# A fused linear attention and gated feed-forward kernel: the attention output x on 64x64 quarters of the array

One core of a Trainium2 chip. The metric is the time of one execution on the device, in microseconds (us); lower is better. The kernel before takes 319.8 us.

## The reference

```python
q_s = softmax(q, axis=-1)                     # [8, 8, 576, 64]: batch, heads, rows, head size
k_s = softmax(k, axis=2)                      # over the rows
kv  = einsum('bhsd,bhse->bhde', k_s, v)       # one 64x64 matrix per head
x   = einsum('bhsd,bhde->bhse', q_s, kv)      # per head, then heads side by side: 4608 x 512
out = (gelu(x @ w_gate) * (x @ w_val)) @ w_out   # 512 -> 1536 -> 512
```

Most of the arithmetic is in the last line. The change concerns `x`, for batches 3 to 7.

## The kernel before

The 576 rows of a batch are split into 512 ("main") and 64 ("left over"; those of all eight batches are run together as a ninth pass). The profile calls the tensor engine PE, its weight loads PEld, VectorE DVE and ScalarE ACT; PSUM is the memory into which matmuls write. Of the tiles named in it, `psg`, `psv` and `psy` are the PSUM results of the gate, value and output products, `pskv` is k times v, `psx` is x of the main rows and `psxr` x of the left-over rows. `eqt` holds the transposed exponentials of q.

Two heads share one full matmul. Their two 64x64 matrices stand on the diagonal of a 128x128 weight, whose other half a mask has set to zero:

```python
def kv_norm(b, g):                      # pskv -> kv_sb, divided by the sums of k, times the mask
    ...
    nc.vector.scalar_tensor_tensor(out=kv_sb, in0=pskv[...], scalar=rck[:, j:j + 1], in1=mask,
                                   op0=ALU.mult, op1=ALU.mult)

def unit_x(b, hp, eng="act", big=False):          # hp: a pair of heads
    xt = get_xt(b)
    psx = (ps_big if big else ps_att).tile([P, MAIN], f32, name="psx", ...)
    nc.tensor.matmul(psx, st[(b, "kv", hp)].rearrange("p h e -> p (h e)"),
                     xq(b, hp), start=True, stop=True)          # 128x128 weight, 512 columns
    copy_on(eng, xt[:, hp, :], psx)

def unit_xrem(b, eng="act"):                      # the 64 left-over columns, four pairs
    psx = ps_att.tile([P, HP, REM], f32, name="psxr", tag="att")
    for hp in range(HP):
        nc.tensor.matmul(psx[:, hp, :], ..., xqr(b, hp), start=True, stop=True)
    copy_on(eng, xtr[:, :, b * REM:(b + 1) * REM], psx)
```

They are placed between the output matmuls of the batch before (`NS, 1` is after the second group of 12 output matmuls, `NS, 12` in the middle of the third, `NS, 2` after it; `FI, 5` and `FI, 7` stand likewise between its gate and value matmuls):

```python
at(b, FI, 5, L(unit_kv, n, 0))
at(b, FI, 7, L(unit_kv, n, 1))
at(b, NS, 1, L(unit_x, n, 0, "dve"), L(unit_x, n, 1, "dve"))
at(b, NS, 2, L(unit_x, n, 2, "act"), L(unit_x, n, 3, "act"))
at(b, NS, 12, L(unit_xrem, n))
```

The softmax here doesn't subtract the row's maximum and nothing guards it: scores larger than these inputs give would overflow.

## Time and profile before

| | before |
|---|---|
| time, median of 4 runs | 319.81 us (319.61 to 320.08) |
| tensor engine (PE) busy | 98% of the span |
| next busiest, VectorE (DVE) | 61% |
| one batch on PE | 33.2 us |
| of that, x: four psx and four psxr | 0.98 us |

The prediction below shows the lines. The time in which PE works on something is read in this document from the first start of it to the first start of what follows; the recorded length of a matmul is not used.

### The profile page before, as it was taken

How to read it: one execution, taken by the hardware profiler on the slowest of the kernel's cores; microseconds unless marked ns; L12 is line 12 of the kernel's file. 1: busy time of each engine (PE TensorE's matmuls, PEld its weight loads, DVE VectorE, ACT ScalarE, POOL GpSimd, SP SyncE). 2: the span in 40 equal slices, each digit the busy share in tenths (PEclk: the TensorE clock that was granted, in tenths of full speed). 3: DMA queues.
4: the chain of work that ended last, by engine and by line, in shares of the span. 5: the costliest groups of instructions: out<-in, count | busy, mean ns of one | idle time of the engine just before them, and what ended most of it. 6: DMA issues, size and time to landing. Idle time of an engine off the chain costs nothing.

```text
span 317.9 us, 4491 instructions
## 1 busy us (share of the span) xinstructions
PE 311.6 (98%) x1658; PEld 148.8 (47%) x1658; DVE 194.1 (61%) x341; ACT 139.8 (44%) x179; POOL 44.7 (14%) x59
## 2 busy tenths in 40 slices
PE   8899999999999999999999999999999999999995
PEld 3444454455545444544454444444444444444444
DVE  3943386698898469747884689457953434234331
ACT  3753565989432753256433653384331233113300
POOL 2667551330004000200003000300000000000000
PEclk9999999999999999999999999999999999999999
DMA  7999999940196118711492139203020210140002
GB/s 231 372 383 395 400 385 388 394 160 0 68 344 215 40 66 268 277 52 66 144 383 70 68 113 386 81 17 132 2 62 22 80 54 0 23 106 6 0 35 99
DMA packets 42342, 50.76 MB, mean 160 GB/s; under 512 B 3408, under 2 KB 38096, under 8 KB 42320
## 3 DMA queue, kind: packets, MB, share of 16 engines
q1 hardware_dynamic: 40592, 48.84, 44.3%
q10 hardware_dynamic: 1728, 1.64, 1.7%
q8 instruction: 13, 0.21, 0.3%
q14 instruction: 9, 0.07, 0.1%
HBM read 37.75 MB, written 9.44 MB: 148 GB/s over the span
## 4 chain that ended last, share of the span: by engine, by line
PE 90%; DMA 4%; ACT 3%; DVE 2%; issue 1%; ACTq 0%
PE psy L436 28%; PE psg L358 27%; PE psv L358 27%; PE pskv L213 2%; DMA out_dram<-yo 2%; PE psx L334 2%; DMA qt<-in_q_dram 2%; PE psl L457 1%; DVE rq L177 1%; ACT eq L150 1%; PE pst L275 1%; DVE eq L186 0%; ACT L363 0%; ACT L150 0%; ACT L353 0%
## 5 line engine op out<-in xcount | busy, mean ns | idle before, releaser
L363 ACT ACTIVATE gl<-psg 128x512 f32<-128x512 f32 x108 | 63.9, 598 | 128.1 <-PE psg L358 125.5
L365 DVE SCALAR_TENSOR_TENSOR ht<-psv,gl 128x512 f16<-128x512 f32 x108 | 72.9, 682 | 63.8 <-PE psv L358 63.2
L358 PE MATMUL psg<-xt,wg_sb 128*128 128x512 f16 x384 | 100.5, 379 | 0.1
L358 PE MATMUL psv<-xt,wv_sb 128*128 128x512 f16 x384 | 100.5, 379 | 0.0
L436 PE MATMUL psy<-wo_sb,ht 128*128 128x512 f16 x420 | 95.6, 379 | 0.0
L358 PEld LDWEIGHTS <-wv_sb 128*128 128x128 f16 x432 | 42.2, 98 | 51.2 <-issue 0.8
L358 PEld LDWEIGHTS <-wg_sb 128*128 128x128 f16 x432 | 41.5, 98 | 47.0 <-issue 0.4
L436 PEld LDWEIGHTS <-ht 128*128 128x128 f16 x420 | 40.5, 98 | 47.1
L485 DVE TENSOR_SCALAR yo<-psy 128x512 f32<-128x512 f32 x30 | 20.6, 689 | 31.3 <-PE psy L436 31.3
L128 POOL CAST v<-vt 128x640 f16<-128x640 f32 x26 | 18.8, 762 | 138.4 <-DMA vt<-in_v_dram 121.4
L167 DVE TENSOR_REDUCE rq<-eq 128x10 f32<-128x640 f16 x28 | 22.7, 812 | 5.4 <-ACT eq L150 5.0
L186 DVE TENSOR_TENSOR eq<-eq,rrq 128x640 f16<-128x640 f16 (+1 forms) x29 | 23.3, 804 | 0.3
L150 ACT ACTIVATE ek<-kt 128x1280 f16<-128x1280 f32 (+1 forms) x11 | 19.1, 1746 | 3.6 <-DMA kt<-in_k_dram 3.6
L150 ACT ACTIVATE eq<-qt 128x2560 f16<-128x2560 f32 (+2 forms) x10 | 18.4, 1862 | 2.3 <-DMA qt<-in_q_dram 2.2
L300 DVE STREAM_TRANSPOSE et<-eq 128x640 f16<-128x640 f16 x20 | 16.9, 845 | 0.7
L130 ACT CAST xt<-psx 128x512 f16<-128x512 f32 x17 | 9.3, 588 | 12.9 <-PE psx L334 12.9
L358 PE MATMUL psg<-xtr,wg_sb 128*128 128x512 f16 x48 | 12.3, 379 | 0.0
L358 PE MATMUL psv<-xtr,wv_sb 128*128 128x512 f16 x48 | 12.3, 379 | 0.0
L350 PE MATMUL pswarm<-warm,ident 128*128 128x512 f16 x34 | 9.9, 452 | 1.4 <-POOL ident masks.py:199 1.4
L213 PEld LDWEIGHTS <-ek 128*128 128x128 f16 x140 | 9.1, 97 | 3.1
L150 ACT ACT_TABLE_LOAD x8 | 10.3, 1283 | 0.6 <-DMA qt<-in_q_dram 0.5
L132 DVE CAST xt<-psx 128x512 f16<-128x512 f32 x15 | 9.7, 681 | 1.2 <-PE psx L334 1.2
(67 smaller groups left out, 133.3 us busy)
## 6 DMA issues: line engine op xcount, KB each, us to landing
out_dram<-yo SPq DMA_DIRECT2D x14, 512.0 KB, 3.1
kt<-in_k_dram SPq DMA_DIRECT2D x7, 640.0 KB, 7.1
vt<-in_v_dram SPq DMA_DIRECT2D x7, 640.0 KB, 8.1
qt<-in_q_dram SPq DMA_DIRECT2D x7, 640.0 KB, 5.8
qt<-in_q_dram SPq DMA_DIRECT2D x8, 512.0 KB, 5.8
eqt<-et SPq DMA_DIRECT2D x80, 40.0 KB, 1.9
wost<-in_moe_w_out_dram SPq DMA_DIRECT2D x6, 512.0 KB, 7.9
kt<-in_k_dram SPq DMA_DIRECT2D x6, 512.0 KB, 7.4
```

The lines of the kernel that those rows point to most:

```text
L128: nc.gpsimd.tensor_copy(out=dst, in_=src)
L150: nc.scalar.activation(out=dst[:, n0:NC, h0 * D:h1 * D].rearrange("p n (h d) -> p h n d", d=D), in_=tiles[(nm, b)][:, h0:h1, n0 * D:NC * D ...
L167: nc.vector.reduce_sum(rq, e, axis=mybir.AxisListType.X)
L186: (nc.gpsimd if eng == "pool" else nc.vector).tensor_tensor(out=e, in0=e, in1=rrq.unsqueeze(-1).to_broadcast((P, n, 2, D)), op=ALU.mult)
L213: nc.tensor.matmul(st[(b, "pskv", g)][:, j, :], ek_b[b % 2][:, n, hp * P:(hp + 1) * P], v16_b[b % 2][:, n, 2 * hp:2 * hp + 2, 0:VW], start ...
L300: nc.vector.transpose(out=et[:, :, hp].rearrange("p c (n i) -> p n c i", i=32), in_=eq_b[b % 2][:, :, hp * P:(hp + 1) * P].rearrange("p n ...
L350: nc.tensor.matmul(ps, ident, warm, start=True, stop=True)
L358: nc.tensor.matmul(ps, w[:, ci, fi * P:(fi + 1) * P], xt[:, ci, :], start=(ci == 0), stop=(ci == HP - 1))
L363: nc.scalar.activation(out=gl, in_=psg, func=ACTF.Gelu)
L365: nc.vector.scalar_tensor_tensor(out=ht, in0=psv, scalar=_H_SCALE, in1=gl, op0=ALU.mult, op1=ALU.mult)
L436: nc.tensor.matmul(psy, hts[fi][:, ns * P:(ns + 1) * P], wo_sb[:, fi, :], start=(fi == 0), stop=(fi == NFI - 1))
L485: nc.vector.tensor_scalar(out=yo, in0=psy, scalar1=1.0 / _H_SCALE, scalar2=None, op0=ALU.mult)
```

## The change

The intent: half of the array multiplies zeros in `unit_x`. Instead, each head gets a quarter of the array, and four heads run at the same time. The two heads of a pair sit on the upper and the lower 64 rows; two pairs take the left and the right 64 columns. How the array is split is called its tiling mode (128*128 and 64*64 in the lines of the trace). So that results come out in the order in which the next product wants them, pairs are now made of heads c and c+4; the exponentials and casts, which copy every element anyway, do that on their way.

```diff
+    def heads(x, b, h0, h1):
+        if b >= T32:                                   # T32 = 3
+            return x.rearrange("p (t c) x -> p c t x", t=2)[:, h0 // 2:h1 // 2]
+        return x[:, h0:h1]
...                                                     # used by exp; cast_v likewise
+    def unit_x4(b):
+        xt = get_xt(b)
+        def go(ps, hp, src):
+            for s in range(2):
+                r, t = slice(64 * s, 64 * s + 64), hp % 2
+                nc.tensor.matmul(ps[s][64 * t:64 * t + 64], st[(b, "kv", hp)][r, s, :], src[r],
+                                 start=True, stop=True)
+        psr = [ps_att.tile([P, 2, REM], f32, name="psxr", tag="att") for _ in range(2)]
+        for hp in range(HP):
+            go([p[:, hp // 2] for p in psr], hp, xqr(b, hp))
+        for s, eng in enumerate(("act", "dve")):
+            copy_on(eng, xtr[:, 2 * s:2 * s + 2, b * REM:(b + 1) * REM], psr[s])
+        for i in range(2):
+            ps = [ps_big.tile([P, MAIN], f32, name="psx", tag="mm") for _ in range(2)]
+            for hp in (2 * i, 2 * i + 1):
+                go(ps, hp, xq(b, hp))
+            for s, eng in enumerate(("act", "dve")):
+                copy_on(eng, xt[:, i + 2 * s, :], ps[s])
...
-                at(b, NS, 1, L(unit_x, n, 0, "dve"), L(unit_x, n, 1, "dve"))
-                at(b, NS, 2, L(unit_x, n, 2, "act"), L(unit_x, n, 3, "act"))
-                at(b, NS, 12, L(unit_xrem, n))
+                at(b, NS, 1, L(unit_x4, n))
```

More of the change, by code (lines that the diff above doesn't have):

```diff
@@ L98 @@
     wo_sb = wpool.tile([P, NFI, C], f16, name="wo_sb")
+    T32 = 3
+    def heads(x, b, h0, h1):
+        if b >= T32:
+            return x.rearrange("p (t c) x -> p c t x", t=2)[:, h0 // 2:h1 // 2]
+        return x[:, h0:h1]
     tiles = {}
@@ L149, in exp @@
         dst = (ek_b if nm == "k" else eq_b)[b % 2]
+        o, i = (("p n (c t d) -> p c t n d", "p c t (n d) -> p c t n d") if b >= T32 else
+                ("p n (h d) -> p h n d", "p h (n d) -> p h n d"))
         nc.scalar.activation(
-            out=dst[:, n0:NC, h0 * D:h1 * D].rearrange("p n (h d) -> p h n d", d=D),
-            in_=tiles[(nm, b)][:, h0:h1, n0 * D:NC * D].rearrange("p h (n d) -> p h n d", d=D),
+            out=dst[:, n0:NC, h0 * D:h1 * D].rearrange(o, d=D, **({"t": 2} if b >= T32 else {})),
+            in_=heads(tiles[(nm, b)], b, h0, h1)[..., n0 * D:NC * D].rearrange(i, d=D),
             func=ACTF.Exp)
     def cast_v(b, h0, h1, eng="pool"):
-        if eng == "pool" and h1 - h0 > 2:
+        if h1 - h0 > 2 and (eng == "pool" or b >= T32):
             for h in range(h0, h1, 2):
-                cast_v(b, h, h + 2)
+                cast_v(b, h, h + 2, eng)
             return
         copy_on(eng, v16_b[b % 2][:, :, h0:h1, 0:D].rearrange("p n h d -> p h n d"),
-                tiles[("v", b)][:, h0:h1, :].rearrange("p h (n d) -> p h n d", d=D))
+                (tiles[("v", b)][:, h0 // 2::4] if b >= T32 else tiles[("v", b)][:, h0:h1]).rearrange(
+                    "p h (n d) -> p h n d", d=D))
     def norm_sum(b, hp, n0=0):
@@ L594 @@
     at(3, FI, 11, L(unit_xrem, 0, "dve"))
-    T32 = 3
     for b in range(2, B):
```

## The prediction

> **What bounds the kernel now.** I read the page's totals first, then the chain that ended last, then the stretch of the trace in which the changed work lies. The totals say that the tensor engine is busy practically all the time, and no other engine is near it:
>
> ```profile
> span 317.9 us, 4491 instructions
> PE 311.6 (98%) x1658; PEld 148.8 (47%) x1658; DVE 194.1 (61%) x341; ACT 139.8 (44%) x179; POOL 44.7 (14%) x59
> ```
>
> The chain that ended last says the same in another way: 90% of it is PE, and the line of x (psx, L334) is 2% of it.
>
> ```profile
> PE 90%; DMA 4%; ACT 3%; DVE 2%; issue 1%; ACTq 0%
> PE psy L436 28%; PE psg L358 27%; PE psv L358 27%; PE pskv L213 2%; DMA out_dram<-yo 2%; PE psx L334 2%; DMA qt<-in_q_dram 2%; PE psl L457 1%; DVE rq L177 1%; ACT eq L150 1%; PE pst L275 1%; DVE eq L186 0%; ACT L363 0%; ACT L150 0%; ACT L353 0%
> ```
>
> A busy PE is not yet a PE at its peak, so the third view is the timeline of PE in one output stage, the one in which x of batch 5 is computed (columns: start, length, instructions):
>
> ```profile
> 174.15 5.34 PE L436 MATMUL psy<-wo_sb,ht 128*128 128x512 f16 x24
> 179.33 0.59 PE L334 MATMUL psx<-eqt,kv_sb 128*128 128x512 f16 x2
> 179.76 1.46 PE L436 MATMUL psy<-wo_sb,ht 128*128 128x512 f16 x6
> 181.05 0.28 PE L341 MATMUL psxr<-eqt,kv_sb 128*128 128x64 f16 x4
> 181.17 1.46 PE L436 MATMUL psy<-wo_sb,ht 128*128 128x512 f16 x6
> 182.47 0.59 PE L334 MATMUL psx<-eqt,kv_sb 128*128 128x512 f16 x2
> 182.90 2.75 PE L436 MATMUL psy<-wo_sb,ht 128*128 128x512 f16 x12
> 185.49 0.81 PE L358 MATMUL psg<-xt,wg_sb 128*128 128x512 f16 x3
> ```
>
> Read starts, not lengths: 24 matmuls of 512 columns from 174.15 to 179.33 are 0.216 us each, while one record lasts 379 ns, because each overlaps the next. From piece to piece there is no gap: the two psx cost 179.76 - 179.33 = 0.43 us, the four psxr 0.12 us, the other two psx 0.43 us. So x of one batch occupies PE for **0.98 us**, and every bit of that is on the path, since PE has nothing idle beside it. The same three pieces with the same distances stand at 112.56, 146.12, 212.54 and 245.75 us. Five batches make 4.9 us, 1.5% of the time. A whole batch checks this: 96 gate and value matmuls and 48 output matmuls at 0.216 are 31.1 us, 20 pskv from 162.64 to 163.21 and again from 166.66 to 167.24 are 1.15 us, and x 0.98 us: 33.2 us, and the window of one batch (174.31 to 207.52) is 33.2 us.
>
> **What the Trainium skill says.**
> (1) "TensorEngine Tiling (Array Packing)", Key Properties: tiles work independently, in weight loads and matmuls; changing the tiling mode drains the tensor engine. Every matmul of the kernel before is 128*128, so its trace can confirm neither; no mode is switched in it.
> (2) "TensorE: Matmul & The Clock Gate", Part 3: matmuls on different tiles overlap, with a span of about one matmul plus some 4 ns for each further tile; four row tiles were measured at 3.07 times, sixteen tiles at 10.6 times. No tiled matmul is in this trace. The same page has a warm 512-column matmul every 216 ns, and this trace has 0.216 us.
> (3) The same page, Fast Weight Load: it needs the full 128 columns; the tiling page adds that column tiling switches it off. A load then takes columns / 1.2 GHz, 53 ns for 64. In this trace a full load is recorded at 98 ns, yet four psxr with their four loads pass in 0.12 us, so loads are pipelined here; without the fast mode this may be worse.
> (4) "Perfetto Trace Analysis", Tensor Engine Instruction: the end of a matmul is an estimate of the profiler. The trace agrees (379 ns against 216 ns from start to start), and their difference, 163 ns, is my measure of how long a drain may last.
>
> **The change, part by part.** For batches 3 to 7 the casts put heads c and c+4 side by side. x of a pair was one 128x128 matmul with a block-diagonal weight, half of whose cells are zeros. It becomes two 64x64 matmuls, one on the upper and one on the lower rows; two pairs fill all four quarters. If four run together, 8 matmuls of 512 columns take the time of two.
> - Removed per batch: 4 psx and 4 psxr, 0.98 us.
> - Added, x itself: two groups of four, 2 x 0.216 = 0.43 us, and about 3 x 0.02 us for the later start of the last tile: 0.49 us.
> - Added, the 64 left-over columns: 8 instead of 4 matmuls. At the 0.03 us of one psxr (0.12 / 4) they look bound by issue and weight loads, not by columns, so I give concurrency nothing here: 8 x 0.03 = 0.24 us. It was 0.12 us.
> - Added, two changes of mode (psy to x, x to psy). A whole drain would be 0.163 us each; part of it should pass beside the next weight load. I choose 0.125 us each, 0.25 us together. This is the least certain term.
> - Sum: 0.49 + 0.24 + 0.25 = 0.98 us, just what was removed. Before the drains it is a gain of 0.25 us per batch, 1.2 us in all.
> - Moved: all of it goes to the end of the second output row group, where the first two psx were. Rotated operands come by the sixteen transposing DMAs, whose issues end at 163.19 + 10.13 = 173.3 us plus 1.9 us to land; x starts at 179.3. For the last batch it is 229.61 + 10.33 + 1.9 = 241.8 against 245.75. No wait there. psxr comes 1.7 us earlier, still behind the data.
> - Buffers: four of the six large PSUM buffers are taken at once. The ring then gives psg and psv of rows 10 and 11, whose readers are done some 5 us before (the last gate product of the batch is at 174.42 + 0.69), and the next output takes the one that was copied out around 177 us. The copies of x end about 3 us before the next batch's first psg at 185.49, so nobody waits for them.
> - Copies: six per batch instead of five (two of 128 columns instead of one of 256, and still two each of 512 on ACT and DVE). DVE gets some 0.3 us more in a stage where it has idle time (0.70 us before the yo at 179.53, 1.35 us before that at 185.69). ACT's exp ends at 179.96, about when the first x is ready, and its copies are then needed by nobody for 5 us. The casts in the new head order have the same elements and counts: exp still takes whole batches (2.33 us), v still goes in 128x640 pieces. All off the path.
>
> **The rivals.** Since PE is bound and nothing else is, the time after is 319.67 + 5 x (X - 0.98), with X what PE spends on x of one batch.
> - Drain costs nothing and the small matmuls overlap too: X = 0.43 + 0.06 + 0.12 = 0.61, -1.9 us, 317.8 us. For it: the page's 4 ns. Against it: the same skill's sentence on the drain.
> - Only two of four run together, say because the two column tiles on the same rows share a stream or the weight loads of 64 columns don't hide (8 x 53 ns = 0.43 us, an estimate from the TensorE page, is as long as the matmuls themselves): X = 4 x 0.216 + 0.24 + 0.33 = 1.43, +2.3 us, 322.0 us. Nothing in this trace speaks against it.
> - No overlap at all: X = 8 x 0.216 + 0.24 + 0.33 = 2.30, +6.6 us, 326.3 us. Against it: the measured speedups on the page.
> - PE waits, as the order of work changed: a PSUM buffer or a DMA as the new bound. The margins above (2 to 5 us) speak against it; a wait of 0.5 us in each batch would make +2.5 us.
> - A larger gain is not there: x removed altogether would give 4.9 us, 1.5%.
>
> **Range and chances.** The sum lands at equal, 319.6 us. Eight in ten I put between the first rival and the second, a little narrower at the bottom because I believe in some drain: 318.0 to 322.2. Faster by over 2% (6.4 us) is impossible by the last bound, unless something unseen moves: 0.01. Slower by over 2% needs no overlap at all, or waits: 0.04. Within 2%: 0.95.
>
> **What would show it.** In the profile after, the psx group should be 64*64, 64x512, twice as many for batches 3 to 7 (40, beside 12 old ones), and PE's timeline should go from psy to psxr, psx and psy without other work between. The distance from the first psxr to the next psy is X: 0.6 to 1.4 us if I am right. Starts of psx that come in bunches of four, a bunch every 0.22 us, prove four at a time; even distances of 0.1 us are pairs, of 0.2 us none. The gap between the last psy before and the first psxr beyond 0.216 us, and that of the last psx to the next psy, are the drains. Gate matmuls and outputs should keep 0.216 us, and a batch outside x its 32.2 us. The prediction is wrong if X is off these numbers, or if PE shows waits on a PSUM copy, on kv_sb or on eqt that were not there.

## The result, and the profile after

| | before | after |
|---|---|---|
| median of 4 runs each | 319.81 us | 318.40 us (318.31 to 318.87) |
| span in the profile | 317.9 us | 316.7 us |
| first start of x to the next psy, batch 5 | (three pieces) 0.98 us | 0.62 us |

The ratio is 0.9958, with a 95% interval of 0.9941 to 0.9976: 1.3 us less. Ratios here are the mean time of one kernel's fast runs over that of the other's fast runs of the same rounds, so not quite the ratio of the medians quoted.

The totals of the page of after:

```profile
span 316.7 us, 4572 instructions
PE 309.7 (98%) x1698; PEld 146.8 (46%) x1698; DVE 195.4 (62%) x346; ACT 138.4 (44%) x179; POOL 44.6 (14%) x59
```

PE is as full as it was and still bounds the kernel. It has 40 more matmuls and is done 1.2 us earlier. The output stage of after in which x of batch 5 is computed (the timeline of PE; start, length, instructions), to be held against the one in the prediction. Two windows of the timeline are put together; the first ends at 179.0, so that it counts only four of the eight psxr:

```profile
173.70 5.34 PE L471 MATMUL psy<-wo_sb,ht 128*128 128x512 f16 x24
178.97 0.22 PE L365 MATMUL psxr<-eqt,kv_sb 64*64 64x64 f16 x4
...
178.97 0.26 PE L365 MATMUL psxr<-eqt,kv_sb 64*64 64x64 f16 x8
179.06 0.60 PE L365 MATMUL psx<-eqt,kv_sb 64*64 64x512 f16 x8
179.59 5.35 PE L471 MATMUL psy<-wo_sb,ht 128*128 128x512 f16 x24
184.78 1.03 PE L393 MATMUL psg<-xt,wg_sb 128*128 128x512 f16 x4
```

The sum can be read off. The 24 psy begin at 173.70 and need 24 x 0.216 = 5.18 us, to 178.88; psxr begins at 178.97, so **0.09 us** is lost on entering. All eight psxr take 179.06 - 178.97 = **0.09 us**. From the first psx to the next psy are 0.53 us, of which two steps of 0.216 are 0.43 us; the rest, **0.10 us**, is lost on leaving. In all 0.71 us where before had 0.98 us: 0.27 us less per batch, 1.35 us in five batches, which agrees with the measured difference. The psx start as the prediction said that four at a time would: in this window four between 179.05 and 179.08, the other four between 179.27 and 179.30. All the rest on PE together has moved by no more than 0.02 us: from the psy that follows x in batch 5 (in before, its first piece) to the same point in the next, after takes 212.55 - 179.59 = 32.96 us and before 212.97 - 179.76 = 33.21 us, 0.25 us more.

The weight loads (PEld) of the same stage show where the two losses lie:

```profile
178.97 0.21 PEld L365 LDWEIGHTS <-kv_sb 64*64 64x64 f16 x16 [0.42 <-issue]
179.59 2.49 PEld L471 LDWEIGHTS <-ht 128*128 128x128 f16 x13 [0.41 <-issue]
```

In before, the loads of the first two psx stand here:

```profile
179.11 0.31 PEld L334 LDWEIGHTS <-kv_sb 128*128 128x128 f16 x2
```

There a load starts well ahead of its matmul (load at 179.11, psx at 179.33). In after the first load of each kind starts only with its own matmul, after some 0.4 us without any load. At each change of mode the overlap is broken.

### The profile page after: what moved, and what is told of

Same layout as the page of the kernel before. It is cut to its first block, busy times and chain, and to the rows that moved or that the text cites. A ratio compares the mean times of both kernels' runs of the same rounds, so it can differ in the third digit from the quotient of the medians.

```text
span 316.7 us, 4572 instructions
## 1 busy us (share of the span) xinstructions
PE 309.7 (98%) x1698; PEld 146.8 (46%) x1698; DVE 195.4 (62%) x346; ACT 138.4 (44%) x179; POOL 44.6 (14%) x59
## 4 chain that ended last, share of the span: by engine, by line
PE 90%; DMA 4%; ACT 3%; DVE 2%; issue 1%; ACTq 0%
PE psy L471 29%; PE psg L393 28%; PE psv L393 28%; PE pskv L226 2%; DMA out_dram<-yo 2%; DMA qt<-in_q_dram 2%; PE psl L492 1%; DVE rq L190 1%; PE psx L365 1%; PE psx L347 1%; ACT eq L162 1%; PE pst L288 1%; DVE eq L199 0%; ACT L398 0%; ACT L162 0%
## 5 line engine op out<-in xcount | busy, mean ns | idle before, releaser
L471 PE MATMUL psy<-wo_sb,ht 128*128 128x512 f16 x420 | 94.3, 379 | 0.0
```

What stands on the lines that cost most here:

```text
L471: nc.tensor.matmul(psy, hts[fi][:, ns * P:(ns + 1) * P], wo_sb[:, fi, :], start=(fi == 0), stop=(fi == NFI - 1))
```

## Experiments

Theory: the gain is four matmuls at the same time on four quarters, less what two changes of mode cost. Rivals: it is the gathering of three pieces into one; it is that a 64x64 matmul is short in itself. Medians of before in the four groups of runs on one chip each are 319.6 to 320.1 us, so ratios are compared.

### The move alone

Full matmuls as before, all at the place where the change has them.

```diff
-at(b, NS, 1, L(unit_x, n, 0, "dve"), L(unit_x, n, 1, "dve"))
-at(b, NS, 2, L(unit_x, n, 2, "act"), L(unit_x, n, 3, "act"))
-at(b, NS, 12, L(unit_xrem, n))
+at(b, NS, 1, L(unit_xrem, n), L(unit_x, n, 0, "act", True), L(unit_x, n, 1, "dve", True),
+   L(unit_x, n, 2, "act", True), L(unit_x, n, 3, "dve", True))
```

> The kernel before, with full 128x128 matmuls, but the four psxr and the four psx of batches 3 to 7 all at the place where the change puts them. Theory (the gain is four matmuls at a time on the quarters): no gain, 319.8 us, ratio 0.999 to 1.001, and psxr plus psx still take 0.98 us from the first start to the next psy. Rival (the gain is from gathering the three pieces in one place): 318.4 us, ratio 0.996.

Measured: 319.71 us, ratio 1.000 (0.9986 to 1.0013). Its PE timeline at the same place:

```profile
177.19 2.32 PE L436 MATMUL psy<-wo_sb,ht 128*128 128x512 f16 x10
179.35 0.28 PE L341 MATMUL psxr<-eqt,kv_sb 128*128 128x64 f16 x4
179.47 1.02 PE L334 MATMUL psx<-eqt,kv_sb 128*128 128x512 f16 x4
180.33 0.59 PE L436 MATMUL psy<-wo_sb,ht 128*128 128x512 f16 x2
```

From 179.35 to 180.33 is 0.98 us, and there is no gap on entering (177.19 + 10 x 0.216 = 179.35). The move gives nothing, and the gaps of after do not come with this place: full matmuls have none there.

### The order of issue

Three kernels issue the same eight psx per batch in other orders, so as to let only two quarters run side by side.

```diff
-for hp in (2 * i, 2 * i + 1):
-    go(ps, hp, xq(b, hp))
+for hp, s in ORDER: ...          # shortened: the same matmul, for pair hp and half s (tile s, hp % 2)
+# e2: (0,0) (0,1) (2,0) (2,1) (1,0) (1,1) (3,0) (3,1)    rows only
+# e3: (0,0) (1,0) (2,0) (3,0) (0,1) (1,1) (2,1) (3,1)    columns only
+# e4: (0,0) (2,0) (1,0) (3,0) (0,1) (2,1) (1,1) (3,1)    each tile twice in a row
```

In these three and in the next three kernels the four PSUM buffers are taken together and the copies stand after all eight psx, where after copies each four.

> The kernel after with the eight psx of a batch in another order: head pair 0, 2, 1, 3, so that only the upper and lower row tiles of one column half can run side by side, and the next two wait for the same two tiles. Theory: four steps of 0.216 us for two, 0.43 us more per batch, 2.2 us in all, 320.6 us, ratio 1.002. Rival (small matmuls pass faster by themselves, or more than four are in flight): 318.4 us, as the kernel after.

> The kernel after with all upper-row matmuls of psx before all lower-row ones, so that only the two column tiles on the same rows can run side by side, each with its own stream of data. Theory: also 0.43 us more per batch, 320.6 us, ratio 1.002. Rival (column tiles on the same rows share one stream, and the speed came from the rows alone): eight steps with an overlap of rows only in the middle, 7 to 8 times 0.216 us, up to 6 us more, 324 us.

> The kernel after with the two matmuls of each quarter right after one another. Theory, with starts in order: the second of a quarter waits for the first, and runs beside the first of the next quarter, so five steps of 0.216 us for two: 0.65 us more per batch, 3.2 us in all, 321.6 us, ratio 1.006. Rival (starts need not be in order, or a quarter need not wait for itself): 318.4 us. Rival (a quarter's second matmul blocks everything until it ends): eight steps, 324.9 us.

Measured: 318.50, 318.71 and 318.72 us; ratios 0.9965, 0.9967 and 0.9965, with intervals between 0.9951 and 0.9981. All three are as fast as after within the interval. The numbers of my theory were missed all three times, and as it stood, a rival's number (318.4 us) had come true. Which one? In e4 the psx of a batch, counted in short stretches (the stretch, its length, then the busy time of PE, with the number of psx that are running by their recorded lengths in brackets; the columns after that are other engines, the clock and DMA):

```profile
179.40:179.45 0.05, 0.00 (x0) 0.00 (x0) 0.00 (x0) 1.00 0.00 0
179.45:179.49 0.04, 0.02 (x4) 0.00 (x0) 0.00 (x0) 1.00 0.00 0
179.49:179.67 0.18, 0.18 (x4) 0.00 (x0) 0.00 (x0) 1.00 0.00 0
179.67:179.70 0.03, 0.03 (x8) 0.00 (x0) 0.00 (x0) 1.00 0.00 0
```

Four start together, and the other four 0.22 us later (the first four are still counted then, as a recorded length is 0.38 us), although the program issues two for each quarter one behind the other. So either the matmuls of different quarters pass one another, or one quarter takes two at once. Only a kernel that uses fewer quarters can tell these apart.

### Fewer quarters

All eight psx of a batch on the two upper quarters, on the two left ones, or on one. Their outputs are wrong, which doesn't matter for the times. The rest is as in after, but for the copies: they stand after all eight psx, and in f2 and f3, where the 64 PSUM partitions of the right columns stay unwritten, those of the left columns are copied twice (8 copies of 64 partitions instead of 4 of 128, on ACT and DVE). The diff is shortened to the choice of quarter.

```diff
-r, t = slice(64 * s, 64 * s + 64), hp % 2
+r, t = slice(0, 64), hp % 2                   # f1, columns only
+r, t = slice(64 * s, 64 * s + 64), 0          # f2, rows only
+r, t = slice(0, 64), 0                        # f3, one tile
```

> Wrong on purpose: all eight psx of a batch on the two upper-row tiles (left and right columns); both results of a pair are then those of the first head. The run before showed that the order of issue does not matter, so here only the set of tiles changes. Theory (each tile works on its own, one matmul of 512 columns at a time, 0.216 us): four steps for eight matmuls, 0.43 us more per batch than after, 2.2 us in all, 320.6 us, ratio to before 1.003. Rival (a 64x64 matmul is simply short): 318.5 us, ratio 0.996.

> Wrong on purpose: all eight psx of a batch on the two left-column tiles (upper and lower rows), each overwriting the result of the other head pair; the copies take the lower 64 PSUM partitions twice, four more copies on each of ACT and DVE per batch at most, off the path. Theory: as with two column tiles, 0.43 us more per batch than after, 320.6 us, ratio 1.003. Rival: 318.5 us.

> Wrong on purpose: all eight psx of a batch on one tile. Theory: eight steps of 0.216 us, 1.30 us more per batch than after, 6.5 us in all, 324.9 us, ratio to before 1.016. Rival (a 64x64 matmul is short): 318.5 us.

Measured: f1 320.63 us, ratio 1.0021 (1.0007 to 1.0034); f2 321.08 us, 1.0031 (1.0018 to 1.0045); f3 325.34 us, 1.0167 (1.0152 to 1.0183). Against the ratio of after, 0.9958, these are 2.0, 2.3 and 6.7 us more; 2.2, 2.2 and 6.5 were expected. The PE timelines of f1, f2 and f3, in this order:

```profile
179.83 0.25 PE L365 MATMUL psxr<-eqt,kv_sb 64*64 64x64 f16 x8
179.92 1.03 PE L378 MATMUL psx<-eqt,kv_sb 64*64 64x512 f16 x8
180.88 1.90 PE L476 MATMUL psy<-wo_sb,ht 128*128 128x512 f16 x8
```

```profile
180.47 1.03 PE L378 MATMUL psx<-eqt,kv_sb 64*64 64x512 f16 x8
181.43 1.47 PE L477 MATMUL psy<-wo_sb,ht 128*128 128x512 f16 x6
```

```profile
181.43 0.26 PE L365 MATMUL psxr<-eqt,kv_sb 64*64 64x64 f16 x8
181.51 1.89 PE L378 MATMUL psx<-eqt,kv_sb 64*64 64x512 f16 x8
183.33 1.04 PE L477 MATMUL psy<-wo_sb,ht 128*128 128x512 f16 x4
```

From the first psx to the next psy are 0.96 us with two quarters (f1 and f2 alike) and 1.82 us with one. Less the 0.10 us on leaving, that is four and eight steps of 0.216 us. A 64x64 matmul of 512 columns takes as long as a full one; the whole gain is that four go at once. Two column halves on the same rows do this as well as two row halves. And as one quarter takes one matmul at a time, the first four starts of e4 can't have been on two quarters: matmuls on different quarters do start out of the order of the program. The semaphores kept with the records say the same: in e4's program, built again from its kernel, only the first and the fifth of the eight psx wait for a PSUM buffer, and in all five batches the records of both are among the first four to start. That was the wrong part in my expectation of e2 to e4, not the concurrency.

### The price of a visit

A visit is here a stretch of 64x64 matmuls between full ones. This kernel does the same x work as after, in three visits instead of one.

```diff
-at(b, NS, 1, L(unit_x4, n))
+at(b, NS, 1, L(unit_x4, n, (0,)))     # four psx
+at(b, NS, 12, L(unit_x4, n, (2,)))    # the left-over columns
+at(b, NS, 2, L(unit_x4, n, (1,)))     # the other four psx
```

> The kernel after with the x work of a batch in three pieces instead of one, at the places of the kernel before: four psx, later the left-over columns, later the other four psx. Nothing else changes. The trace of after shows some 0.09 us on entering the 64x64 mode and 0.10 us on leaving it. Theory (these are paid at every visit): two more visits, 0.38 us more per batch, 1.9 us in all, 320.3 us, ratio to before 1.002: the gain is gone. Rival (the gaps belong to waits on data, not to the mode): 318.5 us, ratio 0.996.

Measured: 321.01 us, ratio 1.0028 (1.0016 to 1.0041), 0.3% above before and 2.2 us above after (by the ratios). The PE timeline:

```profile
179.78 0.41 PE L365 MATMUL psx<-eqt,kv_sb 64*64 64x512 f16 x4
180.12 1.47 PE L472 MATMUL psy<-wo_sb,ht 128*128 128x512 f16 x6
181.52 0.26 PE L365 MATMUL psxr<-eqt,kv_sb 64*64 64x64 f16 x8
181.71 1.47 PE L472 MATMUL psy<-wo_sb,ht 128*128 128x512 f16 x6
183.11 0.41 PE L365 MATMUL psx<-eqt,kv_sb 64*64 64x512 f16 x4
183.45 2.76 PE L472 MATMUL psy<-wo_sb,ht 128*128 128x512 f16 x12
```

Six psy need 1.29 us, from 180.12 to 181.41; psxr starts at 181.52, so entering costs 0.11 us. Four psx need 0.216 us, and the next psy is 0.34 us after them: leaving costs 0.12 us. A visit costs some 0.22 us, two more per batch make 0.45 us, and five batches 2.2 us, as measured. The theory holds, with a price slightly above the 0.19 us read in after. With the three old places kept, the change would have lost.

The packed traces, read to the nanosecond, add that the price of entering is the same everywhere: in every visit of after, of e2 to e4, f1 to f3 and this run, 308 to 310 ns pass from the start of the last full matmul to that of the first small one, some 93 ns over the usual 216, whether psx or psxr comes first. Waits on data would hardly be so equal. (The 0.11 us read above holds 0.01 us more, as the first psy after a visit takes some 226 ns to the next.)

What happens within this price (a drain of the array, the load that could not go ahead, or both) stays open: no run separates them.

### The left-over columns twice

```diff
-go([p[:, hp // 2] for p in psr], hp, xqr(b, hp))
+for _ in range(2):
+    go([p[:, hp // 2] for p in psr], hp, xqr(b, hp))
```

> The kernel after with the eight psxr matmuls of a batch done twice, to measure the term of the left-over columns by itself. The prediction gave 0.03 us to each (0.24 us for eight). The trace of after shows 0.09 us from the first psxr to the first psx, four at a time at about 0.02 us. Theory (four at a time, bound by nothing else): 16 psxr, the first psx 0.15 to 0.19 us after the first psxr. Rival (the first four only came fast because their weights were ready, the rest come at 0.03 us each): 0.3 us or more.

```profile
179.62 0.33 PE L365 MATMUL psxr<-eqt,kv_sb 64*64 64x64 f16 x16
179.77 0.61 PE L365 MATMUL psx<-eqt,kv_sb 64*64 64x512 f16 x8
```

Sixteen take 0.15 us, some 9 ns each, with a weight load for every one. The prediction had given 30 ns.

### The idea carried on: k times v on two column halves

`pskv` wastes half of the array in the same way: each matmul gives the products of two heads with each other, and the mask drops them. In batches 3 to 7 each head now gets 64 columns of the array and 65 columns of v and ones; both groups stand in one visit; the mask is not needed. The diff is shortened: the loops over g and j and the division by the sums of k are left out.

```diff
+for n in range(NC):
+    for s in range(2):
+        nc.tensor.matmul(ps[64 * s:64 * s + 64, j, :],
+                         ek_b[b % 2][:, n, hp * P + 64 * s:hp * P + 64 * s + 64],
+                         v16_b[b % 2][:, n, 2 * hp + s, 0:VW], start=(n == 0), stop=(n == NC - 1))
-at(b, FI, 5, L(unit_kv, n, 0))
-at(b, FI, 7, L(unit_kv, n, 1))
+at(b, FI, 7, L(kv4, n))
```

> The kernel after, with the same idea carried to the product of k and v of batches 3 to 7: each of the 20 pskv matmuls of 130 columns (half of whose results the mask throws away) becomes two of 65 columns on the left and the right column half of the array, and both groups stand in one place. Theory: per batch 20 pairs of 65 columns[...], 0.54 us, plus one visit at 0.21 us (the three-visit run), 0.75 us in place of 1.15 us; 2.0 us less in all, 316.7 us where before is 320.0, ratio 0.990. Rival (40 short loads and matmuls are bound by issue, [...]not by columns): 1.0 us plus 0.21 us, no gain over after, ratio 0.996.

Measured: correct, 316.96 us, ratio to before 0.9910 (0.9897 to 0.9924), faster than both kernels. That is 1.5 us below after by the ratios; 2.0 us had been expected. The PE timeline:

```profile
164.50 1.03 PE L417 MATMUL psv<-xt,wv_sb 128*128 128x512 f16 x4
165.46 0.82 PE L240 MATMUL pskv<-v,ek 128*64 128x65 f16 x40
166.22 1.04 PE L417 MATMUL psg<-xt,wg_sb 128*128 128x512 f16 x4
```

The four psv need 0.86 us, to 165.36: 0.10 us on entering. Then 0.76 us to the next psg. That is 0.86 us where two groups of ten took 1.15 us, 0.29 us less, 1.45 us in five batches. If leaving costs the 0.10 to 0.12 us that it cost at 64x64 (no run shows it for this mode), the 20 pairs took about 0.65 us, 33 ns a pair, not the 27 ns that 65 columns would take at the pace of the full matmuls (0.216 us for 512). What makes up the rest is not shown; the rival's 1.0 us for the forty matmuls is excluded.

## Why the prediction was right, point by point

- **PE bounds the kernel and x is on its path with all it takes.** Right: the difference in x (0.27 us per batch) times five is the difference in time, and the three experiments that added 0.43, 0.43 and 1.30 us per batch gave 2.0, 2.3 and 6.7 us.
- **x itself, 0.49 us.** It took 0.43 us; the 0.06 us for late starts is not seen. Four at a time was right, and shown by the kernels on one and two quarters.
- **Left-over columns, 0.24 us.** It took 0.09 us. This is the term that was mis-sized most: I carried the 30 ns of a full psxr over to quarters and gave concurrency nothing. The sixteen psxr in 0.15 us show that it works on small matmuls too.
- **Changes of mode, 0.25 us.** 0.19 us in after, 0.22 us in the three-visit run. The size was about right, by luck: it was chosen between nothing and the 0.163 us that recorded ends overhang, and no run links the price to these.
- **The sum, 0.98 us, no gain.** It was 0.71 us, a gain of 0.4%. All three terms erred to the same side (by 0.06, 0.15 and 0.06 us). So "no gain" was not what came: the interval of the ratio, 0.9941 to 0.9976, excludes 1. The time, 318.40 us, lay within the range because the range was wide; it is nearer to the first rival (317.8 us: drain free, small matmuls side by side) than to the central number (319.6 us). Half of that rival was right, the small matmuls, and half wrong, as the change of mode does cost.
- **Buffers, copies, DMAs and the new order of heads cost nothing.** Right: from batch 3 on no new wait of PE shows, exp of q takes 2334 ns a batch in both traces, and a cast of v 762 and 761 ns.
- **No overlap, pairs only.** Both fell; as kernels of their own (one and two quarters) they took 325.3 and 320.6 to 321.1 us, where the prediction had given these cases 326.3 and 322.0. The sign it named for pairs, even distances of 0.1 us, was wrong: in f1 the two psx of a pair start within 0.01 us of each other, a pair every 0.22 us.

## What to carry to other kernels

A block-diagonal weight is a sign that array time is lost; tiles gave it back in full here (eight psx took two steps of 0.216 us on four quarters, eight steps on one), but each visit to another tile mode cost 0.2 us here, so gather the small matmuls of a kind into one visit. When PE is full, the price of a piece is the distance between starts around it, and five such pieces gave the change in time here to within 0.2 us. To test for concurrency, take tiles away; changing the order of issue told nothing about it here.

## What the Trainium skill lacked or had wrong

- "TensorE: Matmul & The Clock Gate", Part 3, says that matmuls start and end in program order. With each quarter's two psx issued back to back, four started within 0.04 us and the other four 0.22 us later, while one quarter alone takes 0.216 us for each: starts on different tiles are not in program order. Whether ends are is not shown, as they are modelled.
- "TensorEngine Tiling (Array Packing)", Key Properties, says that a change of mode drains the engine, but not what it costs. Here: 0.09 to 0.11 us on entering 64x64 and 0.10 to 0.12 us on leaving, and 0.09 to 0.10 us on entering 128x64.
- "TensorE: Matmul & The Clock Gate", Part 1, gives a floor of some 25 ns from start to start for small matmuls. Spread over four tiles, sixteen matmuls of 64 columns with their loads passed in 0.15 us, 9 ns each; so it is no floor across tiles. Part 3, which the prediction cites, has some 4 ns from tile to tile; Part 1 does not say that its floor leaves this out.
- The same page, LDWEIGHTS, gives columns / 1.2 GHz for a load, by which 64 columns are an estimated 53 ns; the prediction took this for the time without the fast mode, which the page does not say. The trace of after records 107 ns for one 64x64 load, yet 16 of them started and ended within 0.21 us, and 40 loads of 128x64 within 0.71 us. No page has the rate at which loads on different tiles overlap.
